# Fewer weight loads ahead of attention's last value loads, the last gates stored through SP, the third tile's gather ahead of a scatter, and weight conversions at a later hook

## The chip, the cores and the metric

One core of a Trainium2 chip runs the whole program. Its engines are TensorE (PE in the rows; PEld is its weight load), VectorE (DVE), ScalarE (ACT), GpSimd (POOL) and SyncE (SP), which here only issues DMAs. A suffix q (SPq, ACTq, POOLq) means that engine's instruction queue. The metric is the device time of one execution in microseconds (us), and the time of a kernel is the median of its runs.

## The reference

Three layers in a row, on 2304 tokens of width 512 (float32):

```python
# 1. attention, B,H,S,D = 4,8,576,64, causal, window 64
scores = where(0 <= i - j < 64, scale * q @ k.T, -1e9)
x = softmax(scores) @ v                   # -> N,DM = 2304,512
# 2. gated mixture of experts, E = 8, F = 1024
do = x @ w_skip > 0                       # other tokens pass through
e_idx = argmax(x[do] @ w_gate, axis=1); gate_w = softmax(...)[e_idx]
for e in range(8):                        # top 1
    y[e_idx == e] = gate_w * (relu(x[e_idx == e] @ w1[e]) @ w2[e])
x[do] = x[do] + y
# 3. dense layer, d_ff = 2048
h = x @ w_in
out = where(h >= 1, h, where(h <= -1, 0, (h + 1) ** 2 / 4)) @ w_out
```

## The kernel before, in words

`moe_chain` writes its order out by hand (`manual_schedule`): every engine runs its instructions in the order in which the code issues them, and a wait in front of one holds up all behind it on that engine.

**Attention** runs over 18 tiles of 128 tokens (`t`, `NT = 18`). `stage_s` makes scores and `exp`, `stage_t` transposes the probabilities, `stage_v` (L388) multiplies them by the values in four buffers `vt0` to `vt3` and then issues `load_v` (L305, SP's queue), which refills the two buffers that it has just read. `store_t` (L403) stores the tile to the DRAM buffer `x1`, which holds one row per token and the token's gate behind its 512 numbers. `stage_x`, `stage_l` and `stage_l2` transpose the tile and make the routing logits (`xT`, `pl`, copied by ACT to `ls` for the last three tiles, then `lg`). Groups of three tiles are routed together: `route_a` picks the expert (`m`, `d`, `oh`, and `ex` on ACT), `route_b` ranks the tokens (`rk`), `route_g` takes the gate (`sx`, `gate`) and stores it to `x1`, `route_h` and `route_c` turn ranks into the list of token numbers `idx` and the counts `cnt_i`. The last two groups are written out at the end of the function; `keep_warm(n)` puts `n` spare matmuls between steps, with `n` from `KEEP`.

**Weights.** `load_raws` (L115, L118) loads tiles of 512 KB ("raw") as buffers come free, 4 + 2 of them during attention and 2 more afterwards (`RAWS`), in the order of the list `to_load`; `most[0]` is the number that may be in flight or waiting for use. A raw tile of an expert becomes a pair of rounded halves by `split_pair`: one copy on ACT (L136) and one subtraction on DVE or POOL (L137). Raw tiles of the third layer hold int64 words; `convert_ops` (L167) turns one into floats by five DVE instructions. Eight of them (`EARLY`) are converted during the experts, and `SLOW[e]` to `SLOW[e + 1]` says which ones in expert `e`.

**Experts.** For each expert, `load_x` (L715, an indirect DMA on POOL) gathers 128 rows of `x1`, `ffn` runs the two matrices on them as `ha`, `hb` (L759), `hTp` (transposes, L772) and `y` (L798), three passes each over high and low halves, and `store_x` (L724) scatters the rows back. Each activation's transpose is split by ACT (L131, high half) and DVE (L132, low half `hT` or `mxT`); the low half is read only by the last four of each twelve matmuls. `hooks` name places in an expert's first tile at which other work is issued: "start", "a" (after `hT` 0), "b" (after `hT` 1), and 0, 1, 2, ... along the second half of `y`. `y`'s result goes to `mx` by DVE (L803), behind whatever hook 2 put on DVE. An expert with over 128 tokens has a second tile and one with over 256 a third, under `tc.If`; with these inputs experts 2 and 4 have a second tile, and expert 4 a third. `fetch(e, t)` calls `load_x` for tile `t` of expert `e`.

**The third layer** starts when the last expert's rows are back, and takes over half of the time.

Of the kernel before, what the change touches and what calls it, by code (L numbers as in the profile page):

```python
# [10 lines left out]
F32 = mybir.dt.float32  # L11
# [8 lines left out]
P = 128  # L20
# [9 lines left out]
NT = N // P  # L30
# [14 lines left out]
RAWS = (4, 2, 2)  # L45
# [7 lines left out]
)  # L53
AHEAD_OF_IT = 3

SLOW = (0, 1, 2, 4, 4, 6, 7, 8, 8)
ROUTES = (3, 3, 3, 3, 3, 3)
WARM = 69
WARM_COLUMNS = 108
PUT_OFF = 98  # L60
WGW = 32
AHEAD = 3
KEEP = (14, 20, 80, 6, 36)
PASSES = ((0, 0), (0, 1), (1, 0))
PX_END = {3: "s2", 2: "s1", 1: "s0"}
PL_END = {3: "s2", 2: "s1", 1: "pt0"}
# [3 lines left out]
def moe_chain(  # L70
# [203 lines left out]
    with ExitStack() as actx:  # L274
# [97 lines left out]
        def stage_v(t):  # L372
            if t + 1 < NT:
                os = [psp.tile([P, H, P], F32, tag="o", name=f"o{t}")]
            else:
                os = [psp.tile([P, 4, P], F32, tag=f"pt{k}", name=f"o{t}_{k}") for k in range(2)]
            each = H // len(os)

            pts = [st.pop(("pt", 2 * t + k)) for k in range(2)]
            den = sm.tile([P, H, 1], F32, tag="den", name=f"den{t}")  # L380
            rec = sm.tile([P, H, 1], F32, tag="rec", name=f"rec{t}")
            x = ap2.tile([P, H, D], F32, tag="x", name=f"x{t}", bufs=3)
            for j, o in enumerate(os):
                hs = slice(j * each, (j + 1) * each)
                for h in range(H)[hs]:
                    for k in range(2):
                        half = (h + k) % 2
                        nc.tensor.matmul(  # L388
                            o[k * BLK : (k + 1) * BLK, h - j * each, 0:VW],
                            lhsT=pts[k][:, h // 2, half * BLK : (half + 1) * BLK],  # L390
                            rhs=vt[(2 * t + k) % B][:, h * VW : (h + 1) * VW],
                            start=True, stop=True,
                        )
                nc.vector.tensor_scalar_add(den[:, hs], o[:, :, D : D + 1], 1e-9)
                nc.vector.reciprocal(rec[:, hs], den[:, hs])
                nc.vector.tensor_tensor(x[:, hs], o[:, :, 0:D], rec[:, hs].to_broadcast([P, each, D]), ALU.mult)
            st["x", t] = x.rearrange("p h d -> p (h d)")
            i, b = divmod(2 * t, B)
            load_v(i + 1, b)
            load_v(i + 1, b + 1)  # L400
# [21 lines left out]
        def stage_l(t):  # L422

            xT = st.pop(("xT", t))
            if t + 3 < NT:
                pl = misc[:, 272 : 272 + P]
            else:
                pl = psp.tile([P, 4, P], F32, tag=PL_END[NT - t], name=f"pl{t}")[:, 0]
            for c in range(KD):
                nc.tensor.matmul(  # L430
                    pl[c * WGW : (c + 1) * WGW], lhsT=wg_sb[:, c, :], rhs=xT[:, c, :],
                    start=True, stop=True,
                )
            ls = sm.tile([P, P], F32, tag="ls", name=f"ls{t}", bufs=2)
            if t + 3 >= NT:
                nc.scalar.activation(ls, pl, AF.Copy)
            else:
                nc.vector.tensor_copy(ls, pl)
            st["ls", t] = ls
# [83 lines left out]
            if t + n == NT:  # L523
                st["cn"] = cn

        def route_g(t, n):

            ex = st.pop(("ex", t))
            sx = sm.tile([P, n], F32, tag="sx", name=f"sx{t}")
            nc.vector.tensor_reduce(sx, ex, axis=AX.X, op=ALU.add)  # L530
            gate = sm.tile([P, n], F32, tag="gate", name=f"gate{t}")
            nc.vector.reciprocal(gate, sx)
            nc.scalar.dma_start(
                x1[t * P : (t + n) * P, DM:RW].rearrange("(i p) o -> p (i o)", p=P), gate
            )

# [66 lines left out]
        for t in range(NT - 1):  # L603
            if t >= 3:
                stage_v(t - 3)
            if t >= 2:
                stage_t(t - 2)
            for f in due.pop(t, ()):
                f()
            if t % 2:  # L610
                scale_q(t // 2 + 1)
            stage_s(t)
            most[0] = 1 if t < 3 else 2 if t + 4 < NT else RAWS[0] + RAWS[1]
            (load_q if t % 2 else load_k)(t // 2 + 2)
            if t >= 3:
                store_t(t - 3, nc.scalar)
            if t >= 5:
                stage_l2(t - 5, *of[t - 5][1:])
            if t >= 4:
                stage_l(t - 4)  # L620
            if t >= 3:
                stage_x(t - 3)
            if t >= 5:
                t0, i, n, side = of[t - 5]
                if i == n - 1:
                    route_a(t0, n)
                    for f, l in (
                        (partial(route_b, t0, n, side), 1),
                        (partial(route_h, t0, n), 1),
                        (partial(route_c, t0, n), 3),  # L630
                    ):
                        due.setdefault(t + l, []).append(f)
                    gates[t + 1] = partial(route_g, t0, n)
            if t in gates:
                gates.pop(t)()

            if t:
                load_raws()
            for key in raws:
                since.setdefault(key, t)  # L640

            if t + 2 < NT and splits and since.get(splits[0][1:], t) + 2 <= t:
                work(splits, [pool])
# [9 lines left out]
        stage_l(NT - 5)  # L653
        stage_x(NT - 4)
        stage_v(NT - 3)
        store_t(NT - 3, nc.sync)
        stage_t(NT - 2)
        stage_t(NT - 1)
# [13 lines left out]
        route_a(t0, of[t0][2])  # L672
        end["lg"] = psp.tile([P, 4, P], F32, tag="pt1", name="lg_end")[:, 0, 0 : n * (NE + 1)]
        for f in gates.values():
            f()
        stage_l(NT - 3)
        stage_l(NT - 2)
        stage_l(NT - 1)
# [4 lines left out]
        stage_l2(NT - 2, *of[NT - 2][1:])  # L683
        keep_warm(KEEP[3])
        stage_l2(NT - 1, *of[NT - 1][1:])
        route_g(t0, of[t0][2])
        for f in later:
            f()
        route_a(t1, n)
        route_h(t0, of[t0][2], [n - 1])  # L690
        route_g(t1, n)
        keep_warm(KEEP[0])
        route_b(t1, *of[t1][2:])
        route_h(t1, n)
# [4 lines left out]
    with ExitStack() as ectx:  # L699
# [135 lines left out]
        for e in range(NE):  # L835

            mine = pairs(8 * e + RING - 8, 8 * e + 8)
            nxt = pairs(8 * e + 8, 8 * e + RING)
            if e == 0:
                mine, nxt = [], []  # L840
            elif e + 1 == NE:
                nxt = [("s", u, c) for u, c in EARLY if c % 2 == 0]
            turn = [("c", u, c) for u, c in EARLY[SLOW[e] : SLOW[e + 1]]]
            last = e + 1 == NE
            def second():

                xeT[e, 1] = mp.tile([P, 2, KD, P], F32R, tag="mxT", name=f"mxT{e}_1")
                with tc.If(counts[e] > P):
                    prep(xe[e, 1], f"{e}_1", "mxTl", xeT[e, 1])

            hooks = {
                "start": lambda: work(mine, [dve, dve]),
                "a": lambda: (
                    work(splits, [dve, dve]),
                    work(turn if e else [], [dve]),
                    work(nxt, [dve, dve] if last else [dve]),
                ),
                "b": lambda: (work(splits, [dve]), work(nxt, [dve, dve])),
                0: lambda: None if last else (pre(e + 1, 0), fetch(e + 1, 1)),
                1: lambda: (second(), work(splits, [dve]), work(nxt, [dve, dve])),  # L860
                2: lambda: (work(nxt, [dve]), work(turn, [dve])),
            }
            tile_of(e, 0, hooks)
            store_x(at_of(e, 0), xe[e, 0])
            with tc.If(counts[e] > P):  # L865
                fetch(e, 2)
                tile_of(e, 1)
                store_x(at_of(e, 1), xe[e, 1])
                with tc.If(counts[e] > 2 * P):  # L869
                    pre(e, 2)  # L870
                    tile_of(e, 2)
                    store_x(at_of(e, 2), xe[e, 2])
                    with tc.If(counts[e] > 3 * P):
                        with tc.For_i(0, (counts[e] - (2 * P + 1)) // P, 1) as i:
                            at = mp.tile([P, 1], I32, tag="at", name=f"at{e}", bufs=1)
                            nc.vector.tensor_copy(at, idx[:, bass.ds(i + (e * NT + 3), 1)])
                            x = load_x(at, f"{e}_l", "mxl", 1)
                            if e == NE // 2:
                                keep_warm(PUT_OFF)
                            ffn(e, x, prep(x, f"{e}_l", "mxTl"), f"{e}_l", b0=4)  # L880
                            store_x(at, x)
            if e + AHEAD < NE:
                fetch(e + AHEAD, 0)
# [281 lines left out]
```

## Time and profile before

| | before |
|---|---|
| runs | 702.53, 702.78, 705.35 us; median 702.78 us |
| the profiled execution | 703.17 us, of which its span is 701.5 us and 1.7 us lie around it |
| TensorE busy | 674.2 us (96%) |
| VectorE busy | 425.6 us (61%) |
| ScalarE busy | 385.9 us (55%) |
| GpSimd busy | 90.7 us (13%) |

TensorE is the engine that sets the time: the chain of work that ended last is 55% TensorE, 3% VectorE and 1% ScalarE. What another engine does shows in the time only where TensorE waits for it, and there are 27 us of such waits in the span.

### The profile page before, as it was taken

The page shows a single profiled execution, that of the slowest core. Times are in us where ns is not written, and L with a number is a line of the kernel's source. Part 1 is how long each engine was busy: PE and PEld are TensorE (multiplying, and loading weights), DVE is VectorE, ACT ScalarE, POOL GpSimd, SP SyncE. Part 2 cuts the span into 40 slices and gives each one's busy share as a digit, 9 for nine tenths or more (in the row PEclk, how much of TensorE's full clock was granted, in tenths as well). Part 3 has the DMA queues.
Part 4 walks back from the last instruction along what each step waited for, and adds up shares of the span by engine and source line. Part 5 has one row for each costly group of instructions (what it writes and reads, how often), then busy time and mean ns, then how long its engine had stood idle before and what let it go on. Part 6 is the DMA issues. An engine that isn't in the chain of part 4 may idle for free.

```text
span 701.5 us, 12250 instructions
## 1 busy us (share of the span) xinstructions
PE 674.2 (96%) x4630; PEld 575.6 (82%) x4630; DVE 425.6 (61%) x808; ACT 385.9 (55%) x768; POOL 90.7 (13%) x137
## 2 busy tenths in 40 slices
PE   7999989999998998999999999999999999999997
PEld 6777778776776765987989999999999999999995
DVE  4888864897781799787888854444433433433332
ACT  5887742583751764566766655454444454445443
POOL 3255545222210221000000000000000000000000
PEclk9999998999999999999999999999999999999999
DMA  8999953897891693442333202121300030001001
GB/s 259 288 272 290 307 133 115 289 329 275 267 357 31 205 332 95 172 127 84 121 92 96 69 0 61 31 60 31 91 1 0 1 91 0 1 1 45 1 1 45
DMA packets 34504, 88.83 MB, mean 127 GB/s; under 512 B 6958, under 2 KB 8110, under 8 KB 34420
## 3 DMA queue, kind: packets, MB, share of 16 engines
q1 hardware_dynamic: 26208, 73.82, 34.3%
q10 hardware_dynamic: 5892, 7.35, 3.1%
q0 software_dynamic: 2320, 6.58, 2.8%
q8 instruction: 48, 0.79, 0.5%
q14 instruction: 36, 0.29, 0.1%
HBM read 75.65 MB, written 13.12 MB: 127 GB/s over the span
## 4 chain that ended last, share of the span: by engine, by line
PE 55%; DVE 3%; ACT 1%; issue 1%; ACTq 0%; DVEq 0%
PE h L922 27%; PE po L950 26%; PE spare L1038 1%; PE p2x L912 1%; DVE c L943 1%; DVE c L940 1%; ACT q L933 1%; DVE w L137 1%; DVE gs L941 0%; DVE q L932 0%; DVE x2T L132 0%; ACT q L929 0%; DVE q L936 0%; ACT part L959 0%; ACT w L136 0%
## 5 line engine op out<-in xcount | busy, mean ns | idle before, releaser
L922 PE MATMUL h<-x2T,w 128*128 128x384 f32 x1152 | 218.0, 337 | 1.1 <-DVE x2T L132 0.9
L950 PE MATMUL po<-w,gs 128*128 128x512 f32 x864 | 217.3, 395 | 1.7 <-ACT w L136 0.9
L922 PEld LDWEIGHTS h<-x2T,w 128*128 128x128 f32 x1152 | 204.6, 188 | 10.0 <-DVE x2T L132 1.7
L950 PEld LDWEIGHTS po<-w,gs 128*128 128x128 f32 x864 | 159.5, 188 | 32.3 <-ACT w L136 1.2
L929 ACT ACTIVATE q<-h 128x384 f32<-128x384 f32 x96 | 47.0, 489 | 108.1 <-PE h L922 104.2
L932 DVE TENSOR_SCALAR q<-q 128x384 f32<-128x384 f32 x96 | 34.4, 358 | 98.2 <-ACT q L929 98.0
L936 DVE TENSOR_TENSOR q<-hs,q 128x384 f32<-128x384 f32 x96 | 53.7, 559 | 49.8 <-ACT q L933 49.8
L938 ACT ACTIVATE gs<-q 128x384 fp32r<-128x384 f32 x96 | 50.4, 525 | 60.0 <-DVE q L936 60.0
L941 DVE TENSOR_TENSOR gs<-q,gs 128x384 fp32r<-128x384 f32 x96 | 53.6, 559 | 44.4 <-ACT gs L938 44.4
L136 ACT ACTIVATE w<-raw 128x1024 fp32r<-128x1024 f32 x64 | 65.3, 1056 | 18.7 <-PEq L869 4.7
L798 PE MATMUL y<-w,hT 128*128 128x512 f32 x264 | 70.2, 403 | 4.1 <-DVE hT L132 2.8
L137 DVE TENSOR_TENSOR w<-raw,w 128x1024 fp32r<-128x1024 f32 x55 | 64.8, 1219 | 3.8 <-ACT w L136 1.9
L933 ACT ACTIVATE q<-q 128x384 f32<-128x384 f32 x96 | 50.5, 526 | 22.2 <-DVE q L932 18.6
L798 PEld LDWEIGHTS y<-w,hT 128*128 128x128 f32 x264 | 47.3, 188 | 17.3 <-DVE hT L132 4.5
L349 ACT ACTIVATE pr<-s,nb 128x128 f32<-128x128 f32 x144 | 39.2, 384 | 16.5 <-DVE nb L345 16.5
L931 ACT ACTIVATE hs<-h 128x384 f32<-128x384 f32 x96 | 46.7, 487 | 0.0
L759 PE MATMUL ha<-w,mxT 128*128 128x512 f32 x132 | 35.3, 416 | 3.7 <-ACT mxT L131 1.5
L759 PEld LDWEIGHTS ha<-w,mxT 128*128 128x128 f32 x132 | 25.1, 197 | 13.2 <-issue 4.5
L759 PE MATMUL hb<-w,mxT 128*128 128x512 f32 x132 | 35.2, 402 | 0.0
L345 DVE TENSOR_REDUCE nb<-s 128x4 f32<-128x512 f32 x36 | 23.2, 686 | 16.0 <-PE s L338 14.5
L724 POOL DMA_INDIRECT x<-mx,idx x11 | 16.5, 1501 | 115.6 <-POOLq L865 60.4
L131 ACT ACTIVATE hT<-hTp 128x512 fp32r<-128x512 f32 x22 | 13.2, 599 | 27.1 <-PE hTp L772 13.0
(170 smaller groups left out, 702.1 us busy)
## 6 DMA issues: line engine op xcount, KB each, us to landing
raw<-in_wu SPq DMA_DIRECT2D x61, 512.0 KB, 6.0
raw<-in_wd SPq DMA_DIRECT2D x31, 512.0 KB, 4.0
x<-x SPq DMA_DIRECT2D x22, 256.0 KB, 3.2
vt<-in_vs SPq DMA_DIRECT2D x36, 130.0 KB, 6.2
out<-out SPq DMA_DIRECT2D x36, 128.0 KB, 2.4
x<-x ACTq DMA_DIRECT2D x17, 256.0 KB, 6.6
q<-in_qs SPq DMA_DIRECT2D x8, 512.0 KB, 5.0
kt<-in_ks SPq DMA_DIRECT2D x8, 512.0 KB, 6.2
```

Source lines behind the costliest of these rows:

```text
L136: nc.scalar.activation(t[:, 0], src, AF.Copy)
L137: eng.tensor_tensor(t[:, 1], src, t[:, 0].bitcast(F32), ALU.subtract)
L759: nc.tensor.matmul(ph, lhsT=xT[:, a, c, :], rhs=halves[4 * e + j, c][:, b, :], start=(n == 0), stop=(n == len(seq) - 1),)
L798: nc.tensor.matmul(py, lhsT=hT[j][:, a, c, :], rhs=halves[4 * e + 2 + j, c][:, b, :], start=(j == 0 and n == 0), stop=(j == 1 and n == len ...
L922: nc.tensor.matmul(ph, lhsT=halves[U_IN + m // 4, c][:, b, (m % 4) * P : (m % 4 + 1) * P], rhs=xT[:, a, c, :], start=(n == 0), stop=(n == ...
L929: nc.scalar.activation(q, ph, AF.Relu, bias=0.5, scale=0.5)
L931: nc.scalar.activation(h, ph, AF.Copy)
L933: nc.scalar.activation(q, q, AF.Square)
L936: nc.vector.tensor_tensor(q, h, q, ALU.max)
L938: nc.scalar.activation(gs[:, 0], q, AF.Copy)
L941: dve.tensor_tensor(gs[:, 1], q, gs[:, 0].bitcast(F32), ALU.subtract)
L950: nc.tensor.matmul(po[i], lhsT=gs[:, a, i * P : (i + 1) * P], rhs=w[:, b, :], start=(m == m0 and (a, b) == PASSES[0]), stop=(m == m1 - 1 a ...
```

## The change

Five edits, the last in several lines. In the code: the limit on raw tiles in the last attention tiles goes from 8 to 3, and the larger limit holds only after `stage_v(NT - 3)`; the last three gates are stored by SP and no longer by ACT, the gate of the last group but one is made after `route_a` of the last, `ls` has three buffers for two, and four spare matmuls go; `fetch(e, 2)` moves from behind the first tile's scatter to hook 1; all conversions of an expert stand at hook 2 (before, those of experts 1 to 7 were split between hook "a" and hook 2), and the numbers of conversions in experts 0 to 7 become 2, 1, 2, 0, 2, 1, 0, 0 where they were 1, 1, 2, 0, 2, 1, 1, 0. The warm-up at the start has 73 matmuls of 102 columns for 69 of 108 (7446 and 7452 columns).

```diff
-SLOW = (0, 1, 2, 4, 4, 6, 7, 8, 8)
+SLOW = (0, 2, 3, 5, 5, 7, 8, 8, 8)
-WARM = 69
-WARM_COLUMNS = 108
+WARM = 73
+WARM_COLUMNS = 102
-KEEP = (14, 20, 80, 6, 36)
+KEEP = (10, 20, 80, 6, 36)
...
-            ls = sm.tile([P, P], F32, tag="ls", name=f"ls{t}", bufs=2)
+            ls = sm.tile([P, P], F32, tag="ls", name=f"ls{t}", bufs=3)
...
-        def route_g(t, n):
+        def route_g(t, n, eng=nc.scalar):
...
-            nc.scalar.dma_start(
+            eng.dma_start(
                 x1[t * P : (t + n) * P, DM:RW].rearrange("(i p) o -> p (i o)", p=P), gate
             )
...
-            most[0] = 1 if t < 3 else 2 if t + 4 < NT else RAWS[0] + RAWS[1]
+            most[0] = 1 if t < 3 else 2 if t + 3 < NT else 3
...
         stage_v(NT - 3)
+        most[0] = RAWS[0] + RAWS[1]
+        load_raws()
         store_t(NT - 3, nc.sync)
...
         for f in gates.values():
-            f()
+            f(eng=nc.sync)
...
-        route_g(t0, of[t0][2])
         for f in later:
             f()
         route_a(t1, n)
+        route_g(t0, of[t0][2], nc.sync)
         route_h(t0, of[t0][2], [n - 1])
-        route_g(t1, n)
+        route_g(t1, n, nc.sync)
         keep_warm(KEEP[0])
...
                 with tc.If(counts[e] > P):
                     prep(xe[e, 1], f"{e}_1", "mxTl", xeT[e, 1])
+                    fetch(e, 2)
...
                 "a": lambda: (
                     work(splits, [dve, dve]),
-                    work(turn if e else [], [dve]),
                     work(nxt, [dve, dve] if last else [dve]),
                 ),
...
-                2: lambda: (work(nxt, [dve]), work(turn, [dve])),
+                2: lambda: (work(nxt, [dve]), work(turn, [dve] * len(turn))),
...
             with tc.If(counts[e] > P):
-                fetch(e, 2)
                 tile_of(e, 1)
```

How the program's order moves at three places follows. On SP's queue, near the end of attention, the value loads (`vt`) and raw loads (`raw`) stand so before:

```order
L305 DMA vt2_160<-in_vs 64x520
L305 DMA vt3_161<-in_vs 64x520
L115 DMA raw4_2_1631<-in_wu 128x1024
L115 DMA raw5_0_1633<-in_wu 128x1024
L115 DMA raw5_2_1635<-in_wu 128x1024
L115 DMA raw6_0_1637<-in_wu 128x1024
L305 DMA vt0_158<-in_vs 64x520
L305 DMA vt1_159<-in_vs 64x520
L115 DMA raw6_2_1731<-in_wu 128x1024
```

and so in the changed kernel:

```order
L305 DMA vt2_160<-in_vs 64x520
L305 DMA vt3_161<-in_vs 64x520
L305 DMA vt0_158<-in_vs 64x520
L305 DMA vt1_159<-in_vs 64x520
L115 DMA raw4_2_1727<-in_wu 128x1024
L115 DMA raw5_0_1729<-in_wu 128x1024
L305 DMA vt2_160<-in_vs 64x520
L305 DMA vt3_161<-in_vs 64x520
L115 DMA raw5_2_1838<-in_wu 128x1024
```

Four raw loads stood ahead of the next pair of value loads, and now none; the last three of the eight raw loads have gone behind the last value loads. On ScalarE, at the end of attention, where the last three tiles' logits are copied (`ls`), the rows before are:

```order
L474 ACTIVATE ex1_137<-d12_2092 128x3x8
L533 DMA x1_68<-gate9_2105 128x3x1
L436 ACTIVATE ls15_2113<-pl15_2108 128x128
L436 ACTIVATE ls16_2120<-pl16_2115 128x128
L436 ACTIVATE ls17_2127<-pl17_2122 128x128
L533 DMA x1_68<-gate12_2161 128x3x1
L474 ACTIVATE ex2_138<-d15_2169 128x3x8
L533 DMA x1_68<-gate15_2185 128x3x1
```

and in the changed kernel:

```order
L474 ACTIVATE ex1_137<-d12_2096 128x3x8
L436 ACTIVATE ls15_2117<-pl15_2112 128x128
L436 ACTIVATE ls16_2124<-pl16_2119 128x128
L436 ACTIVATE ls17_2131<-pl17_2126 128x128
L474 ACTIVATE ex2_138<-d15_2168 128x3x8
```

The three gate stores are gone from ScalarE; they are the last three DMAs on SP's queue now. On VectorE, in expert 2 from the first `hT` to the second tile's, the rows before are (`c` and `raw` are a conversion's):

```order
L132 TENSOR_TENSOR hT2_0_0_3354<-hTp2_0_0_3349,hT2_0_0_3354 128x512
L167 TENSOR_SCALAR c32_2_3357<-raw32_2_2934 128x512
...
L137 TENSOR_TENSOR w12_0_3365<-raw12_0_2967,w12_0_3365 128x1024
L132 TENSOR_TENSOR hT2_0_1_3390<-hTp2_0_1_3385,hT2_0_1_3390 128x512
...
L137 TENSOR_TENSOR w14_2_3445<-raw14_2_3325,w14_2_3445 128x1024
L167 TENSOR_SCALAR c32_2_3357<-raw32_3_2962 128x512
...
L803 SCALAR_TENSOR_TENSOR mx2_0_2395<-y2_0_3378,mx2_0_2395 128x512
L865 COMPARE_AND_BRANCH
L132 TENSOR_TENSOR hT2_1_0_3499<-hTp2_1_0_3494,hT2_1_0_3499 128x512
```

and in the changed kernel:

```order
L132 TENSOR_TENSOR hT2_0_0_3362<-hTp2_0_0_3357,hT2_0_0_3362 128x512
L137 TENSOR_TENSOR w12_0_3365<-raw12_0_3004,w12_0_3365 128x1024
L132 TENSOR_TENSOR hT2_0_1_3390<-hTp2_0_1_3385,hT2_0_1_3390 128x512
...
L137 TENSOR_TENSOR w14_2_3448<-raw14_2_3333,w14_2_3448 128x1024
L167 TENSOR_SCALAR c32_2_3019<-raw32_3_2962 128x512
...
L167 TENSOR_SCALAR c33_0_3460<-raw33_0_2967 128x512
...
L805 SCALAR_TENSOR_TENSOR mx2_0_2395<-y2_0_3378,mx2_0_2395 128x512
L867 COMPARE_AND_BRANCH
L132 TENSOR_TENSOR hT2_1_0_3507<-hTp2_1_0_3502,hT2_1_0_3507 128x512
```

The conversion that stood between the two `hT` has gone from there, and two stand in a row ahead of the first tile's `mx` and the second tile's `hT`. In expert 1 one conversion moves the same way, and in expert 0 a second one joins the one at hook 2.

## Rows read from the trace of the kernel before

**Rows 1.** Windows: length, busy us (instructions) by engine, granted clock PEclk, DMA share.

```profile
84.70:97.65 12.95, 10.77 (x205) 9.19 (x206) 8.85 (x30) 6.79 (x21) 3.43 (x8) 1.00 0.79 206
97.65:115.06 17.41, 15.49 (x202) 14.51 (x201) 10.10 (x42) 4.86 (x10) 10.00 (x14) 0.80 0.17 47
...
228.70:271.30 42.60, 39.03 (x176) 29.51 (x176) 38.27 (x45) 30.23 (x38) 8.94 (x12) 1.00 0.68 228
...
282.20:701.50 419.30, 411.59 (x2090) 371.11 (x2088) 216.19 (x412) 220.55 (x448) 0.00 (x0) 1.00 0.17 50
```

**Rows 2.** Timeline of PE: start, length, instruction [idle before <-releaser].

```profile
85.95 0.30 PE L388 MATMUL o<-vt,pts 128*64 128x65 f32 x2 [1.26 <-DMA vt<-in_vs]
86.54 1.15 PE L388 MATMUL o<-vt,pts 128*64 128x65 f32 x30 [0.28 <-DMA vt<-in_vs]
```

**Rows 3.** Timeline of SP's queue: start, time from first issue to last.

```profile
71.84 5.65 SPq L115 DMA_DIRECT2D raw<-in_wu  x4
77.59 1.51 SPq L305 DMA_DIRECT2D vt<-in_vs  x2
```

**Rows 4.** The DMA issued at 77.59: size, us from issue to landing.

```profile
vt<-in_vs SPq DMA_DIRECT2D x1, 130.0 KB, 8.2
```

**Rows 5.** Timeline of ACT at the routing of the last tiles.

```profile
101.66 0.38 ACTq L533 DMA_DIRECT2D x<-gate  x1
102.08 0.45 ACT L436 ACTIVATE ls<-pl 128x128 f32<-128x128 f32 x2 [1.42 <-DVE ps L514]
```

**Rows 6.** Timeline of PE at the same place.

```profile
99.90 0.95 PE L430 MATMUL pl<-xT,wg_sb 128*32 128x128 f32 x24
...
102.41 0.91 PE L449 MATMUL lg_end<-quarters,ls 128*128 128x9 f32 x4 [0.78 <-ACT ls L436]
```

**Rows 7.** Timeline of DVE at the same place.

```profile
104.34 0.18 DVE L457 TENSOR_REDUCE m<-lg_end 128x3 f32<-128x24 f32 x1 [1.51 <-PE lg_end L449]
...
106.97 0.18 DVE L512 TENSOR_TENSOR r<-rk_end,oh 128x27 f32<-128x27 f32 x1 [0.39 <-PE rk_end L509]
```

**Rows 8.** Windows, as rows 1, in the third tile.

```profile
216.00:217.00 1.00, 1.00 (x3) 0.79 (x3) 0.00 (x0) 0.00 (x0) 0.00 (x0) 0.50 0.00 0
```

**Rows 9.** Timeline of PE, expert 4's third tile and expert 5's first.

```profile
213.19 0.63 PE L733 MATMUL mpx<-ident,mx 128*128 128x128 f32 x4 [1.75 <-DMA mx<-x,idx]
214.50 4.60 PE L759 MATMUL ha<-w,mxT 128*128 128x512 f32 x12 [0.69 <-ACT mxT L131]
...
228.71 3.05 PE L759 MATMUL ha<-w,mxT 128*128 128x512 f32 x12 [0.43 <-PEq L873]
```

**Rows 10.** Timeline of POOL: gathers of experts 2 and 4, and a scatter.

```profile
152.30 1.12 POOL L715 DMA_INDIRECT mx<-x,idx  x1 [0.22 <-issue]
...
207.11 1.02 POOL L724 DMA_INDIRECT x<-mx,idx  x1 [13.10 <-DVE mx L803]
...
208.43 0.98 POOL L715 DMA_INDIRECT mx<-x,idx  x1 [0.24 <-issue]
```

**Rows 11.** Timeline of DVE: conversions, and what follows them.

```profile
128.83 0.43 DVE L167 TENSOR_SCALAR c<-raw 128x512 int32<-128x512 int32 x1 [0.24 <-DVEq L848]
...
131.70 0.74 DVE L803 SCALAR_TENSOR_TENSOR mx<-y,mx 128x512 f32<-128x512 f32 x1
...
135.85 0.69 DVE L132 TENSOR_TENSOR hT<-hTp,hT 128x512 fp32r<-128x512 f32 x1 [0.83 <-ACT hT L131]
...
150.85 0.68 DVE L132 TENSOR_TENSOR hT<-hTp,hT 128x512 fp32r<-128x512 f32 x1
...
151.90 1.42 DVE L167 SCALAR_TENSOR_TENSOR c<-raw,c 128x512 int32<-128x512 int32 x2
```

**Rows 12.** Timeline of PE: value products y of experts 2 and 4.

```profile
151.28 1.62 PE L798 MATMUL y<-w,hT 128*128 128x512 f32 x6
...
167.17 3.96 PE L798 MATMUL y<-w,hT 128*128 128x512 f32 x16 [0.81 <-DVE hT L132]
...
207.48 3.96 PE L798 MATMUL y<-w,hT 128*128 128x512 f32 x16 [0.82 <-DVE hT L132]
```

## The prediction, made before the changed kernel ran

> **What bounds the kernel now.** I read the page first: TensorE is busy for 674.2 of 701.5 us, so an edit helps only where TensorE waits or runs at a lowered clock. Then I cut the span into stages with the windows view. The third layer's window is 419.30 us long with 411.59 of TensorE's work [rows 1], and no edit reaches it. Of the waits before it, the timeline of TensorE shows four places that the change touches. First, near attention's end it stands for 1.26 and 0.28 us for value loads [rows 2]. Second, the routing of the last tiles is a chain of short steps between ACT, TensorE and DVE, and its window has a mean granted clock of 0.80 [rows 1]. Third, expert 4's third tile waits 1.75 us for its gather and 0.69 for the split behind it, and its first twelve matmuls take 4.60 us where expert 5's take 3.05 [rows 9]; the clock in that tile is 0.50, which is 1.2 of 2.4 GHz [rows 8]. Fourth, the second tiles of experts 2 and 4 wait 0.81 and 0.82 us for DVE's `hT` [rows 12]. The changed order on DVE acts on the last.
>
> **Term 1, value loads: -1.55.** The pair of loads that TensorE waits for was issued at 77.59 and took 8.2 us to land; ahead of it in SP's queue stand four raw loads, 2 MB, issued from 71.84 to 77.49 [rows 3, 4]. The changed order has none of the four ahead, so the load goes out as soon as its buffer is read, up to 5.65 us earlier, and without that 2 MB in front of it. To remove the whole wait it must land 1.55 us earlier [rows 2]. The raw loads that go behind are used after attention only. I take all of it; the lower bound of the gain is nothing, if SP still comes late.
>
> **Term 2, routing: -1.2 (from -0.6 to -1.9).** `pl` is done at 100.85 (99.90 + 0.95) [rows 6], but ACT copies it to `ls` only at 102.08, since a gate store in its queue stands until 101.66 for DVE's gate [rows 5]; TensorE waits 0.78 us for that copy [rows 6] and DVE then 1.51 us for TensorE, until 104.34 [rows 7]. With the store gone and a third `ls` buffer, the copies can run at 100.9 to 101.7, and the logits are ready 0.75 us earlier at the clock of now. If the clock does not fall, since that 0.78 us wait is gone, each spare and logit matmul on the way takes half as long, and the first step of `route_a` comes at 102.8, 1.5 us earlier. Behind it `route_g` of the group before (two DVE steps of 0.2) now stands ahead of `r`, but DVE has 0.39 us of waiting in front of `r` [rows 7], which covers it, and four spare matmuls less save up to 0.4. The gates through SP go out in DVE's order, and nothing stands behind them on SP but the loads of the experts. Bounds: 0.6 with the clock lowered, 1.9 with full clock to the gather. I take the middle, as one of the two waits that precede the low clock goes and the other stays.
>
> **Term 3, the third tile: -3.0.** The gather of 208.43 stands behind the scatter of 207.11, which waits 13.10 us for DVE's `mx` [rows 10]. At hook 1 the gather goes out over 10 us earlier, behind the gathers for the next experts. So the wait of 1.75 goes, less about 0.3 for the branch that stays as at 228.71 (0.43 there) [rows 9]: -1.45. With no such gap the clock has no reason to fall in this tile, and the 1.55 us (4.60 - 3.05) return: -1.55. Lower bound -1.45, if the 0.69 us behind it alone lower the clock. The gather now runs while DVE works. The row that shows that case is the gather of 152.30, beside a conversion of 151.90: 1.12 us for 0.98 [rows 10, 11], and the conversion's pair took 1.42 us, so 0.14 us on POOL and nothing on DVE, hidden by the 10 us. The Trainium skill (SBUF — State Buffer, section "SBUF: two separate sides") speaks against the move: a DMA issued from GpSimd has its descriptors written there, and a DVE operation that holds the port pair which they share shuts it out until it ends. By that rule the gather could be held for a whole conversion step; even so its row would land before the tile needs it, and the sum would stay.
>
> **Term 4, conversions: +2.0 in expert 2, +0.8 in expert 4, 0 in experts 5 to 7.** One conversion takes 2.87 us on DVE (128.83 to 131.70) [rows 11]. Expert 0 has one more, so `mx` and all that follows on DVE comes 2.87 later. At 135.85 DVE had 0.83 us of idle time [rows 11], which takes part of it: 2.04 us late. In expert 1 the conversion leaves hook "a" and comes back at hook 2, so that at its end DVE is again 2.04 late. The first low half in expert 2 is then done at 150.85 + 0.68 + 2.04 = 153.57. TensorE reads it with the ninth matmul of `y`, two matmuls into the group of 151.28 (1.62 us for six) [rows 12], at 151.8: a new wait of 1.7 us. Expert 2 has no conversion at "a" any longer, so the later waits for `hT` and `mxT` in this tile go, but two stand ahead of the second tile's `hT`. That comes 2.0 us later than before, and TensorE waited for it already [rows 12], so the stage ends 2.0 us later. Upper bound: 2.87, if the idle time isn't recovered. In expert 4 both conversions stand at hook 2. DVE reaches hook 2 earlier by up to the conversion that has left "a", so the delay at 207.48 lies between nothing and 2.87; I take 0.8, nearer to nothing, since only what DVE can't do earlier, for want of its inputs, remains. In experts 5 to 7 DVE is busy for 38.27 of 42.60 us and TensorE idle for 3.57 [rows 1]: one conversion moves later in expert 5 (a wait of about 1 us at the start of expert 6's `y`), and the one of expert 6 is gone, which gives about as much back. I take 0, from -1.0 to +1.0.
>
> **The rest: 0.** The warm-up has 7446 columns for 7452. Splits stand where they stood.
>
> **Sum.** -1.55 - 1.2 - 3.0 + 2.0 + 0.8 = -2.95, from 703.17 us (span 701.5 and 1.67 around it) to 700.2. The profiled execution is 0.39 above the median of the runs, so against 702.78 it is 699.85; I say 699.9. The smallest difference that can be told is about 0.5%, 3.5 us: faster lies below 699.3, slower above 706.3.
>
> **Rivals.** (A) is the forecast, 40%: 698.6 to 701.2.
>
> (B) The conversions cost nothing, 28%. DVE has idle time in each expert that I counted only once, and with the last conversions gone from expert 6 the waits there shrink. Then only terms 1 to 3 count, -5.75: 697.0, and with the full gain in term 2 some 696.3. For it: DVE is 61% busy over the span. Against it: TensorE already waits for DVE at both second tiles [rows 12].
>
> (C) The other side, 22%: the new waits lower the clock. Term 4 makes waits of 1.7 and about 2 us where none exceeded 0.82, and the trace has one such case: 1.75 and 0.69 us with 0.63 of work between, after which the clock was 0.50 and the twelve matmuls lost 1.55 us [rows 8, 9]. One such loss gives 701.4, two 703.0, three 704.5; the kernel is slower than before (702.8) from the second on. Against it: the waits of 1.26 and 0.28 us [rows 2] lie in a window with a mean clock of 1.00 [rows 1].
>
> (D) The value loads still come late, 5%: three raw loads behind one another share the DMA engines with the last pairs, and the wait comes back there: 701.4.
>
> (E) The routing gains nothing, 5%: the last gate, through SP, lands after the index list and holds the first gather, which takes what term 2 gave: 701.1.
>
> From these: A is below 699.3 in about a third of its range, B always, so faster 0.41; slower only with three losses in C and a second mishap, 0.03; same 0.56. The range from B's lower end to two losses in C: 696.3 to 703.0.
>
> **What would show it.** Right: no wait for `vt` over 0.5 us before the last pair; `ls` right after `pl`; the third tile's `mpx` straight after the second tile's `y`, and its twelve `ha` matmuls in 3.05 us; a wait of about 1.7 us early in expert 2's `y`, and one of about 2 us in its second tile, both for DVE's `hT`. Wrong: a granted clock below 1.00 in expert 2 or behind (C), waits in expert 2 no longer than before (B), `mpx` of the first tile later against `idx` than now (E).

## The result, and the profile after

The changed kernel takes 707.29 us in the median of 20 runs (701.66 to 711.5), the kernel before 702.75 in 20 runs; the ratio is 1.0054 with a 95% interval of 1.0033 to 1.0074. So it is slower by about 3.8 us by the ratio (4.5 by the medians), where 2.9 us less was forecast. The profiled execution took 708.03 us with a span of 706.3.

The gains that were forecast are in the trace. TensorE's timeline of the changed kernel no longer has the waits of [rows 2]: the same products run without a gap, and only the very last loads are waited for, as before.

```profile
86.80 1.16 PE L388 MATMUL o<-vt,pts 128*64 128x65 f32 x32
...
97.24 1.12 PE L388 MATMUL o<-vt,pts_last 128*64 128x65 f32 x30 [0.50 <-DMA vt<-in_vs]
```

The third tile's rows on TensorE (line numbers are two higher) show the gather's wait gone and the twelve matmuls at 3.07 us, against [rows 9]:

```profile
218.39 0.60 PE L735 MATMUL mpx<-ident,mx 128*128 128x128 f32 x4
219.68 3.07 PE L761 MATMUL ha<-w,mxT 128*128 128x512 f32 x12 [0.69 <-ACT mxT L131]
```

What was lost stands elsewhere. First, the routing itself is done earlier, but the gather does not follow. In SP's queue, POOL's timeline and TensorE's timeline of the changed kernel:

```profile
94.78 1.01 SPq L115 DMA_DIRECT2D raw<-in_wu  x2
95.88 0.39 SPq L118 DMA_DIRECT2D raw<-in_wd  x1
96.36 3.48 SPq L403 DMA_DIRECT2D x<-x  x3
102.35 3.78 SPq L533 DMA_DIRECT2D x<-gate  x3
```

```profile
111.82 1.23 POOL L717 DMA_INDIRECT mx<-x,idx  x1 [3.94 <-issue]
```

```profile
115.64 0.63 PE L735 MATMUL mpx<-ident,mx 128*128 128x128 f32 x4 [2.81 <-DVE w L137]
117.08 4.60 PE L761 MATMUL ha<-w,mxT 128*128 128x512 f32 x12 [0.81 <-ACT mxT L131]
```

The kernel before had at this place, on TensorE:

```profile
115.09 0.63 PE L733 MATMUL mpx<-ident,mx 128*128 128x128 f32 x4 [0.64 <-DVE w L137]
116.53 3.05 PE L759 MATMUL ha<-w,mxT 128*128 128x512 f32 x12 [0.81 <-ACT mxT L131]
```

The three raw loads went out ahead of the last three `x` stores, these ahead of the gates, and the last gate, issued at 105.77, took 4.9 us to land, until 110.67; POOL, done with its routing work at 107.9, stood 3.94 us before it gathered at 111.82. The profile names nothing that released it ("issue"), so that it was the gate is inferred from these times. The gather took 3.6 us to land, and TensorE waited 2.81 us where the kernel before waited 0.64; its first twelve matmuls took 4.60 us for 3.05. Second, the second tiles of experts 2 and 4 wait for DVE's low half `hT`, as named, 2.32 and 2.35 us where about 2 and 1.6 were forecast. There are also waits at the start of `y` in experts 2 and 6. TensorE's timeline in experts 2, 4 and at the start of 6:

```profile
153.65 1.66 PE L800 MATMUL y<-w,hT 128*128 128x512 f32 x6 [0.95 <-issue]
...
171.66 5.55 PE L800 MATMUL y<-w,hT 128*128 128x512 f32 x16 [2.32 <-DVE hT L132]
...
214.59 3.97 PE L800 MATMUL y<-w,hT 128*128 128x512 f32 x16 [2.35 <-DVE hT L132]
...
253.15 1.65 PE L800 MATMUL y<-w,hT 128*128 128x512 f32 x6 [1.28 <-ACT hT L131]
```

Sixteen matmuls took 5.55 us behind the first wait of 2.3 us and 3.97 behind the second. The first and the last of these four rows are not the wait that was forecast: TensorE stands there ahead of the first six matmuls of `y` (the forecast named the ninth), which read the high half of ACT. ACT's timeline at the two places:

```profile
153.00 0.60 ACT L131 ACTIVATE hT<-hTp 128x512 fp32r<-128x512 f32 x1 [2.40 <-DVEq L867]
252.50 0.60 ACT L131 ACTIVATE hT<-hTp 128x512 fp32r<-128x512 f32 x1 [3.15 <-DVEq L867]
```

ACT waited for the branch in DVE's instruction queue (line 867), which stands behind hook 2's conversion and `mx` (on DVE from 152.09 in the first case), and its high half was done at 153.60, just before the matmuls began at 153.65. The windows view has the granted clock, the third number from the end, at 0.50 at three places:

```profile
118.00:120.00 2.00, 2.00 (x6) 1.58 (x5) 0.00 (x0) 0.00 (x0) 1.02 (x2) 0.50 0.91 219
173.00:175.00 2.00, 2.00 (x6) 1.57 (x5) 0.00 (x0) 0.00 (x0) 0.00 (x0) 0.50 0.61 232
...
323.00:325.00 2.00, 2.00 (x6) 1.60 (x5) 2.00 (x4) 1.11 (x2) 0.00 (x0) 0.50 0.00 0
```

The last of these lies in the third layer, which the change does not touch. A reader who compares only these two traces would charge it to the change; the traces of the other kernels say how far that is right.

### The profile page after: what moved, and what is told of

The parts are those of the page before. It is cut to its first block, busy times and chain, and to the rows that moved or that the text cites. A ratio compares the mean times of both kernels' runs of the same rounds, so it can differ in the third digit from the quotient of the medians.

```text
span 706.3 us, 12264 instructions
## 1 busy us (share of the span) xinstructions
PE 674.3 (95%) x4630; PEld 573.9 (81%) x4630; DVE 426.2 (60%) x808; ACT 385.6 (55%) x768; POOL 89.3 (13%) x137
## 4 chain that ended last, share of the span: by engine, by line
PE 51%; DVE 6%; ACT 2%; issue 1%; ACTq 0%; DVEq 0%
PE po L951 25%; PE h L923 24%; DVE c L944 2%; PE spare L1039 1%; ACT q L934 1%; DVE gs L942 1%; PE p2x L913 1%; DVE c L941 1%; DVE w L137 1%; DVE q L933 1%; DVE q L937 1%; DVE x2T L132 0%; ACT q L930 0%; ACT gs L939 0%; DVE c_first L944 0%
## 5 line engine op out<-in xcount | busy, mean ns | idle before, releaser
L800 PE MATMUL y<-w,hT 128*128 128x512 f32 x264 | 71.8, 411 | 7.8 <-DVE hT L132 4.7
L131 ACT ACTIVATE hT<-hTp 128x512 fp32r<-128x512 f32 x22 | 13.2, 598 | 28.7 <-PE hTp L774 12.1
```

Of the source, the lines that this page charges most:

```text
L800: nc.tensor.matmul(py, lhsT=hT[j][:, a, c, :], rhs=halves[4 * e + 2 + j, c][:, b, :], start=(j == 0 and n == 0), stop=(j == 1 and n == len ...
```

## The experiments

Each kernel was timed in turn with the kernel before, 12 runs in most. The mean granted clock of the runs is given, since it turned out to matter; it is 0.993 to 0.994 for the kernel before.

| kernel | ratio to before, 95% interval | mean clock |
|---|---|---|
| the changed kernel | 1.0054 (1.0033 to 1.0074) | 0.990 |
| after_again: the same | 1.0026 (0.9999 to 1.0053) | 0.992 |
| fetch_alone | 0.9981 (0.9952 to 1.0011) | 0.993 |
| conv_alone | 1.0031 (1.0001 to 1.0060) | 0.993 |
| route_alone | 1.0008 (0.9980 to 1.0036) | 0.993 |
| raws_alone | 0.9999 (0.9973 to 1.0026) | 0.992 |
| raws_and_route | 0.9972 (0.9948 to 0.9996) | 0.994 |
| raws_after_gates | 1.0048 (1.0024 to 1.0072) | 0.990 |
| old_conv | 0.9940 (0.9917 to 0.9963) | 0.995 |
| best_mix | 0.9964 (0.9941 to 0.9987) | 0.993 |
| no_fetch | 1.0023 (0.9998 to 1.0048) | 0.994 |
| numbers_only | 0.9957 (0.9936 to 0.9979) | 0.995 |
| hook_only | 1.0049 (1.0025 to 1.0073) | 0.992 |
| hook2_in_2 | 0.9972 (0.9949 to 0.9994) | 0.993 |
| hook2_in_4 | 0.9975 (0.9950 to 0.9999) | 0.994 |
| conv_and_fetch | 1.0019 (0.9996 to 1.0042) | 0.992 |
| filled | 1.0177 (1.0140 to 1.0214) | 0.989 |

Two theories stood first. Theory gates: the raw loads, stores and gates in one queue delay the first gather, and that is the loss. Theory conversions: the waits for `hT`, with the clock behind them, are the loss.

**One part alone** (each is the hunks of the diff above, on the kernel before). fetch_alone:

> The kernel before with the third tile's gather at hook 1 as its only edit. Both theories (the loss lies in the conversions' new waits; the loss lies in the gates behind the raw loads on SP) leave this part alone: the third tile's wait of 1.75 us and its low clock go, -3.0 us, about 699.8 against 702.8. If the gather among DVE's work costs something that the whole change hid, less than 1.5 us is gained.

conv_alone:

> The kernel before with only the numbers of conversions and their hook changed. Theory conversions: the waits for hT in experts 2 and 4 that the changed kernel shows (2.32 and 2.35 us) come here too, +3 us, and +1.5 for each lowered clock: 705.5 to 708. Theory gates: the waits are there but the clock falls less often, since the gather at the start is not late: +2 to +3, about 705. If the conversions are hidden when they stand alone: 702.8.

route_alone:

> The kernel before with only the routing edits: gates through SP, three ls buffers, the gate of the last group but one later, four spare matmuls less. The raw loads stand where they stood. Theory gates: with no raw loads ahead of the last x stores the gates land before 109 and the first gather goes out at about 109.8 for 111.2, the clock stays full in the routing: -1.5 to -3, about 700.5. Rival (SP's gate stores are slow in themselves): they land after 110 here too, the first gather is no earlier than 111.2, and nothing is gained: 702.8 or more.

raws_alone:

> The kernel before with only the limit on raw tiles and the later load_raws. The wait for vt of 1.5 us goes in both theories. Theory gates: the last x stores land at about 108 behind the three raw loads, but the gates, on ACT, land no later than about 110, so the first gather stays at 111.2 and the gain in attention becomes a longer wait there: -0.5 to 0, 702.3 to 702.8. Rival (the late stores alone cost nothing): -1.5, 701.3.

The gather alone: 702.21 us against 703.14; the forecast of 3 us less is at the edge of the interval. The routing: 702.75, nothing gained, as its rival expected, though its gather goes out 10.0 us after the last `x` store (100.47 to 110.48) where the kernel before took 12.4 (98.82 to 111.22). But raws_alone has the routing code of before and took 10.9 (96.91 to 107.80), with a full clock in this stretch. The windows view has, in the kernel before and then in raws_alone:

```profile
98.80:111.20 12.40, 11.09 (x134) 10.64 (x133) 6.61 (x35) 4.33 (x10) 5.19 (x9) 0.72 0.11 23
96.90:107.80 10.90, 8.41 (x134) 7.70 (x133) 6.65 (x35) 4.31 (x10) 5.57 (x11) 1.00 0.49 135
```

So most of the 2.4 us went with the clock of one execution, and what the edits give is about 1 us. The raw loads alone: 702.08 in the median, a ratio of 0.9999, inconclusive. The conversions: 704.43, slower, by about the 2 us that theory gates allowed them. In their trace, the third tile's wait is the one of [rows 9], yet the matmuls behind it run at full clock; TensorE's timeline and the window there:

```profile
214.17 0.63 PE L733 MATMUL mpx<-ident,mx 128*128 128x128 f32 x4 [1.73 <-DMA mx<-x,idx]
215.49 3.05 PE L759 MATMUL ha<-w,mxT 128*128 128x512 f32 x12 [0.69 <-ACT mxT L131]
```

```profile
216.00:218.00 2.00, 2.00 (x10) 1.59 (x10) 0.16 (x1) 0.00 (x0) 0.00 (x0) 1.00 0.04 8
```

The same two waits, 1.73 and 0.69 for 1.75 and 0.69, had a clock of 0.50 behind them in [rows 8]. So this wait is not always followed by a low clock. Six of the traces here have it (the gather behind the scatter, 1.64 to 1.86 us): the twelve matmuls took 4.38 to 4.60 us in three of them and 3.05 to 3.07 in three. In the twelve traces without it they took 3.06 or 3.07 each time. The wait belongs to the code, and whether the clock falls behind it to the execution.

**The late gates.** raws_after_gates moves the late `load_raws` behind the gates:

```diff
-        most[0] = RAWS[0] + RAWS[1]
-        load_raws()
         store_t(NT - 3, nc.sync)
...
         route_g(t1, n, nc.sync)
+        most[0] = RAWS[0] + RAWS[1]
+        load_raws()
         keep_warm(KEEP[0])
```

> The changed kernel with the three raw loads that stand ahead of the last x stores on SP moved behind the three gate stores. Theory gates: from the issue of the last x store to the first gather it took 12.3 us in the changed kernel and 10.0 with the routing edits alone; it goes back to about 10, the wait of 2.81 us before the first expert and the low clock behind it go: -2.3 and about -1.2, 703.5 to 704 where the changed kernel has 707.3. Theory conversions: the loss is in experts 2 and 4, nothing changes here: 706.5 to 707.3. Rival: the raw loads now run beside the gather and hold it as long.

raws_and_route has the two edits that meet on SP and no other:

> The kernel before with the raw loads' limit and the routing edits, and nothing else. Theory gates: the two edits do together what neither does alone: the gates wait on SP behind raw loads and x stores, the first gather comes 12 us after the last x store for 10 to 11 with either alone, +1.5 to +2.5 against each alone: 703.5 to 705. Rival (parts add up): 701.5 to 702.5.

Theory gates fell in both. With the loads behind the gates the gather did go out early, 10.06 us after the last store (97.94 to 108.00), but TensorE waited for it nearly as long, and the twelve matmuls behind took 4.60 us again, as POOL's and TensorE's timelines show:

```profile
108.00 1.23 POOL L717 DMA_INDIRECT mx<-x,idx  x1 [1.77 <-DVE cnt_i L573]
```

```profile
113.61 0.63 PE L735 MATMUL mpx<-ident,mx 128*128 128x128 f32 x4 [2.43 <-issue]
115.05 4.60 PE L761 MATMUL ha<-w,mxT 128*128 128x512 f32 x12 [0.81 <-issue]
```

From the gather's issue to `mpx` it is 5.6 us here and 3.8 in the changed kernel, with three raw loads issued just ahead, which may have held it (its landing is not on record there): what the gates gave, the gather lost, and the time stayed at 707.02. And raws_and_route, with the late gates, is faster than before (700.10). Still, a cost of the two edits together shows: in all twelve traces that have both, TensorE waits 0.91 to 2.81 us ahead of the first expert, and in six of them the first matmuls behind are slow (4.60 us or more); in the six other traces it waits 0.49 to 0.75, and none is slow.

**The conversions.** old_conv is the changed kernel with these lines as before:

```diff
-SLOW = (0, 2, 3, 5, 5, 7, 8, 8, 8)
+SLOW = (0, 1, 2, 4, 4, 6, 7, 8, 8)
...
+                    work(turn if e else [], [dve]),
...
-                2: lambda: (work(nxt, [dve]), work(turn, [dve] * len(turn))),
+                2: lambda: (work(nxt, [dve]), work(turn, [dve])),
```

> The changed kernel with the conversions as before (numbers and hooks). Theory conversions: all of the loss goes with them, 702.8 or less. Theory gates: only what the conversions cost alone goes, about 1.8 us by the runs so far, and the late gather stays: about 705.

It is the fastest kernel of all, 698.66 us against 702.71, in the range of theory conversions and far below the other: theory conversions holds. (The changed warm-up, which was not run alone, is in this kernel too and so is not the loss.) best_mix is the kernel before with the gather, the routing and the raw loads behind the gates:

> The kernel before with the early third gather, the routing edits, and the raw loads behind the gates; conversions and warm-up as before. Theory gates: the gains of the parts alone are there together: -1.4 for the gather, -1.2 for the value loads, up to -1 for the routing, 699 to 700.5 against 702.8 to 703. Rival (raw loads beside the first gather cost as much as they gain): 701.5 or more.

It took 700.37: the gains are there without the conversions, though no more than in old_conv. Beside raws_after_gates, which differs from it by the conversions and the warm-up alone, it is 6.7 us faster. Which half of the conversions' edit costs? numbers_only has the new `SLOW` but the line at "a"; hook_only the old `SLOW` without it.

> The changed kernel with the new numbers of conversions, but the first of an expert at hook a again (two at hook 2 in expert 0). Theory: of the waits, those of the second tiles come from two conversions in a row ahead of hT; with one at hook a the second tiles wait 0.8 us as before, and only the one more conversion before expert 1 is late: about 1 to 2 us above the kernel with the old conversions, 700 to 701. Rival (the earlier conversion itself costs): 704 or more.

> The changed kernel with the old numbers of conversions, all of an expert at hook 2. Theory: experts 2 and 4 still have two in a row, so their second tiles wait over 1.5 us and the clock falls there: 3 to 6 us above the kernel with the old conversions, 702 to 705. Rival (the numbers carry the loss): 699 to 700.

The numbers cost little (700.41) and the hook about all of it (705.27, just above its forecast). In numbers_only, TensorE's timeline has the second tiles' waits as before the change:

```profile
170.79 3.95 PE L800 MATMUL y<-w,hT 128*128 128x512 f32 x16 [0.80 <-DVE hT L132]
...
211.14 3.95 PE L800 MATMUL y<-w,hT 128*128 128x512 f32 x16 [0.82 <-DVE hT L132]
```

hook2_in_2 and hook2_in_4 keep the pair at hook 2 in one expert (`turn if e not in (0, 2)`, or `(0, 4)`, at "a").

> The changed kernel with one conversion back at hook a in experts 1, 3, 4, 5; only expert 2 keeps both at hook 2. Theory waits and clock: expert 2's second tile waits 2.3 us, the clock falls behind it in some runs, 2 to 3.5 us above the kernel with the new numbers and hook a (699.8 in the mean): 702 to 703.3. Rival (expert 4 carries the loss): about 700.

> The same with expert 4 alone keeping both conversions at hook 2. Theory: its second tile waits 2.3 us, 1.5 to 3 us above 699.8: 701.3 to 703. Rival (expert 2 carries the loss): about 700.

They took 700.23 and 701.67 us; the first is at its rival's number, the second in its forecast. By the ratios each is about 1 us above numbers_only, which the intervals do not tell from nothing, and each has one wait of 2.42 or 2.34 us. Neither expert carries the loss alone. TensorE's timeline at expert 2's second tile in hook2_in_2, and then in conv_alone:

```profile
167.04 5.54 PE L800 MATMUL y<-w,hT 128*128 128x512 f32 x16 [2.42 <-DVE hT L132]
```

```profile
167.19 3.95 PE L798 MATMUL y<-w,hT 128*128 128x512 f32 x16 [2.32 <-DVE hT L132]
```

Eight of the traces here have this wait (2.30 to 2.43 us). The sixteen matmuls behind it took 5.53 to 5.55 us in four of them and 3.95 or 3.96 in four; in the ten traces with a wait of 0.84 us or less they took 3.94 to 3.96. Behind the wait in expert 4's second tile (2.34 or 2.35 us in eight traces) they took 3.94 to 3.97 every time. What is left up to the changed kernel was not separated further: both pairs together, and the moves in experts 1 and 5.

**The gather and the conversions together.**

> The changed kernel with the third tile's gather behind the scatter as before. Theory conversions (their waits cost about 3 us wherever they stand, the rest is the clock): the gain of the gather goes, 1.4 to 3 us, so 708 to 709.5. Rival (the conversions cost more in the whole change than alone because the early gather meets them on DVE and POOL): the loss shrinks to about 1.8 us over raw loads and routing together, 702.5 to 703.

> The kernel before with the conversions' numbers and hook and the early gather, nothing else. If the early gather and the conversions at hook 2 disturb each other: slower than the conversions alone (704.8 in the mean), 705.5 or more. If the two add up: the conversions' +1.7 and the gather's -1.4, about 703.4.

no_fetch took 704.52 and conv_and_fetch 704.32, each between its two forecasts. So beside all the other edits the early gather does not help by these runs, while conv_and_fetch is no slower than the conversions alone; a gain of 1.4 us is within the intervals in the second case and hardly in the first. The traces show no wait that the gather adds: TensorE's waits from 140 to 275 us (over 0.2 us) are 10.0 us in conv_and_fetch and 12.1 in conv_alone, 10.0 in the changed kernel and 12.7 in no_fetch. Nor do the runs show that the gather alone makes the conversions dearer. By differences of the ratios they cost 2.2 us alone, 2.7 with the gather, 3.6 with raw loads and routing (no_fetch less raws_and_route), and 6 to 8 with all three, each to within 2 to 3 us.

**Filling the waits.** filled is the changed kernel with spare matmuls in the waits:

```diff
-KEEP = (10, 20, 80, 6, 36)
+KEEP = (10, 20, 105, 6, 36)
...
+                    if j == 0 and n == 8 and name in ("2_1", "4_1"):
+                        spare = bank(7, [P, 4, P], "spare")
+                        for _ in range(9):
+                            nc.tensor.matmul(
+                                spare, lhsT=ones,
+                                rhs=ones.rearrange("p (o k) -> p o k", o=1).to_broadcast([P, 4, P]),
+                                start=True, stop=True,
+                            )
```

> The changed kernel with nine spare matmuls of 512 columns (0.25 us each) where TensorE waits for hT in the second tiles of experts 2 and 4, and 25 more of 128 columns ahead of the first expert; all fit into waits that are there. Theory clock: the waits stay, but TensorE is busy in them, the low clock behind them goes: one to two low stretches of some 1.5 us fewer, 704 to 705.5 for 706.7. Rival (the waits alone are the loss): no change in time, 706.5 to 707.5.

It took 713.78 us and settles nothing. The waits for `hT` shrank to 0.4 us and the clock stayed at 1.00 behind them, but TensorE now waits for its own instruction queue at the start of experts, 3.61 us in the longest case where the changed kernel has 0.43 at such places:

```profile
147.93 5.42 PE L761 MATMUL ha<-w,mxT 128*128 128x512 f32 x12 [3.61 <-PEq L875]
```

**The changed kernel again**, beside three of the others:

> The changed kernel as it is, beside the three others on one chip. If the loss belongs to the code: 706 to 707.5, with more lost clock than the kernel before. If the first measurement was the chip's: within 1.5 us of the kernel before.

It took 705.20 for 702.82, a ratio of 1.0026, in neither of the two ranges; alone it would not settle the question. hook_only and raws_after_gates, with the conversions at hook 2, are slower than before clear of noise, old_conv is faster: the loss is the code's, and its size differs between executions. The trace of after_again has the waits of 2.31 and 2.35 us, and yet a span of 699.1, with a clock lower only at one place in the third layer and at the end. Of the 7.2 us to the first trace, 4.2 are there when the first expert's rows come (111.47 for 115.64), with the clock at 1.00 in both up to 110.

## Why the prediction was wrong

**Term 1 held in its waits.** The 1.55 us of waits are gone. In time it can't be told alone (raws_alone).

**Term 2 was mis-sized.** The chain became faster as described, but some 1.5 us of the 2.4 between the two traces (12.4 to 10.9 with the old code) was the granted clock, which the old code also has at full in other executions. What was left came back: the first gather went out 12.3 us after the last `x` store in the changed kernel, by the times above because the gates came late through SP. That is rival E, with a longer wait than it was given, and the way out that was tried (raws_after_gates) only moved the wait to the gather.

**Term 3: the wait held, its clock did not.** The 1.75 us are gone in every trace with the early gather. The 1.55 us of low clock came in three of the six traces that have this wait, and the prediction counted them as if they came always. So the term was nearer to its lower bound of 1.45, and alone it measured 0.9 by the medians, with an interval from 3.4 us less to 0.8 more.

Without the conversions, terms 1 to 3 measured -4.0 us (old_conv, 702.71 to 698.66) for the -5.75 of rival B.

**Term 4 held in the sum of its waits and failed in their price.** All waits over 0.2 us of TensorE between 140 and 275 us, added up from its timeline, are 6.9 us in old_conv and 10.0 in the changed kernel (10.4 in its second trace): +3.1 to +3.5 for the +2.8 forecast. Between conv_alone and the kernel before it is 12.1 and 9.0, the same 3.1. In expert 2 the sum came out (+2.0) though one path was wrong: the early wait is 0.95 us and not 1.7, and by the times above it comes through DVE's branch and ACT's high half, not DVE's low half. In expert 4 it is +1.3 for 0.8.

But in time the conversions cost about 8.6 us in the whole change (707.29 to 698.66), 6.5 with the second measurement, and 6.7 between raws_after_gates and best_mix. The step that failed is the choice of case A over case C: that the new waits would leave the clock alone and cost no more than their length. In four of eight traces the clock fell behind the wait in expert 2, at 1.6 us each time. The mean clock of the runs is 0.9898 in the changed kernel (0.9921 the second time) and 0.9952 in old_conv; over a span of 705 us that is 3.8 us of lost clock more (2.2). Fitted over all runs of all kernels here, each kernel with a level of its own, a microsecond of lost clock goes with about 0.65 us of time: 2.5 us (1.4). Waits and clock together make 5.6 us of the 8.6 (4.9 of 6.5). Where the clock was alike the waits are nearly all: the traces of after_again and old_conv, both at 0.997, have spans of 699.1 and 695.9, 3.2 us apart. So rival C's mechanism was there, at one of its two places and in half of the traces. The time lies above the range because the gains were 1.7 us smaller and the conversions 5.8 us dearer than forecast, and C's losses were set against the gains in full.

What stays open: the other 3 us of the first measurement (1.6 of the second), and why the early gather gained nothing beside the conversions and the other edits. Alone, the conversions cost 2.2 us by their ratio, from 0.1 to 4.2, so the 3.1 us of added waits are all that is needed there, and their clock was that of the kernel before (0.993). The four traces with a low clock in expert 2 are all of kernels that have raw loads, routing and early gather too (four of five such traces, none of the other three). That may be why the conversions cost more there, but it was noticed afterwards, and no run isolates it.

## What to carry to other kernels

A stretch of low clock in one trace is no fixed property of the code: the stretches looked at here came behind waits, and behind the same wait in some executions and not in others. Before crediting an edit with it, look how many executions have it at that place, and price a new or a removed wait by its length plus that share of the lost clock. Work that an in-order engine does later delays all that follows on it, branches too, and other engines that wait for these. Two conversions in a row ahead of `hT` cost more here than one at each of two places. When a store is moved to another queue, list what is ahead of it there, with landing times.

## What was not expected of the hardware

The third layer of every kernel has the same three short waits (0.91 to 0.94, 0.89 to 0.92 and 0.75 to 0.77 us), and behind them the clock fell in eight of the eighteen traces. TensorE's timeline in the changed kernel, and then in no_fetch:

```profile
317.76 2.01 PE L923 MATMUL h<-x2T,w 128*128 128x384 f32 x10 [0.93 <-DVE x2T L132]
320.68 0.50 PE L951 MATMUL po<-w,gs 128*128 128x512 f32 x1 [0.91 <-ACT w L136]
321.94 3.35 PE L951 MATMUL po<-w,gs 128*128 128x512 f32 x8 [0.76 <-DVE w L137]
```

```profile
315.78 2.01 PE L923 MATMUL h<-x2T,w 128*128 128x384 f32 x10 [0.94 <-DVE x2T L132]
318.70 0.50 PE L951 MATMUL po<-w,gs 128*128 128x512 f32 x1 [0.91 <-ACT w L136]
319.96 2.11 PE L951 MATMUL po<-w,gs 128*128 128x512 f32 x8 [0.76 <-DVE w L137]
```

The waits agree to 0.01 us, and the eight matmuls took 3.35 and 2.11 us. Among the 20 runs of the changed kernel, the fastest took 701.66 us at a mean clock of 0.996, the one with the lowest clock (0.984) 708.11, and the slowest 711.5 at 0.987: the clock goes with the time, but does not account for all of it.
